# Forgetting attention with a gelu feed-forward block: row-tiled causal masks, a reordered batch 0, and batch 1 in the steady order

## The chip, the cores and the metric

The kernel runs on one core of a Trainium2 chip. The metric is the device time of one execution in microseconds (us), median of several executions. Before the change it is 352.60 us (four runs beside those of the changed kernel, 352.09 to 354.32).

## The reference, cut to what matters

```python
# q, k, v: (8 batches, 8 heads, 576 tokens, 64); f: (8, 8, 576)
cum    = cumsum(log(clip(f, 1e-4, 1)))
scores = q @ k.T / 8 + cum[:, None] - cum[None, :]      # causal: -1e9 above the diagonal
x      = (softmax(scores) @ v), as (4608 tokens, 512)
h      = x @ w_in                                        # (512, 2048)
out    = (0.5 * h * (1 + erf(h / sqrt(2)))) @ w_out      # exact gelu; w_out (2048, 512)
```

So each batch needs attention, a first product with gelu, and a second product. The decay by f is folded into v (a weight for each token), so the scores need only the causal mask.

## The kernel before

Heads are handled in pairs (HP = 4 pairs a batch). The scores of a pair are four tiles of up to 448 columns per head, each followed by one exponential on ScalarE. TensorE interleaves batch b's attention with single products of batch b-1's second product ("fill"). From batch 2 on, q and k are transposed by DMA; batches 0 and 1 transpose them on TensorE, because their loads come too late for that.

The causal mask is put on by TensorE itself in batch 0 and for pair 0 of batch 1: a 128-row product of the identity with a mask tile opens the accumulation, and the score piece is cut in two around the masked 128 columns. Elsewhere GpSimd masks after the exponential.

```python
def scores(b, i, t):
    on_pe = b == 0 or (b == 1 and i == 0)
    for x, c in enumerate(SDIAG[t] if on_pe else []):        # masked columns of this tile
        for h in range(2):
            nc.tensor.matmul(st[:, h, c:c+P], ident_bf, after, start=x == 0, stop=False)
    for n, q0, w in STILES[t]:
        cut = P if on_pe and c in SDIAG[t] and w > P else w
        for a0, a1 in ((0, cut), (cut, w)):
            for h in range(2 if a1 > a0 else 0):             # two heads on 64 rows each
                nc.tensor.matmul(st[:, h, c+a0:c+a1], kT[i][d, ...], qT[i][d, ...], ...)
    nc.scalar.activation(et, st, Act.Exp, scale=scale)
```

One block of transposes for a pair of heads of batch 1 is twelve TensorE transposes (q, then k, two 64-wide tokens side by side) and eight VectorE copies out of PSUM, four for qT and then four for kT:

```python
def transposes_pe(b, i, pool):
    for src, ps in zip(qk_of[b], pss):                       # q, then k
        for h in range(2):
            for j in range(JT // 2):
                nc.tensor.transpose(ps[:, h, j, :], src[:, 2*i+h, 2*j*D:2*(j+1)*D], ...)
    for which, ps in enumerate(pss):                         # qT, then kT
        for h in range(2):
            for odd in range(2):
                nc.vector.tensor_copy(rows[:, odd], ps[odd*D:(odd+1)*D, h]...)
```

Before, three of these blocks stand in batch 0's first product and the fourth early in batch 1's attention. The first quarter of w_out is loaded after batch 0's attention, the other three in the middle of its first product.

The softmax here doesn't subtract the row's maximum and nothing guards it: scores larger than these inputs give would overflow.

## Time and profile before

| what | value | from |
|---|---|---|
| median of the timed runs | 352.60 us | 4 runs |
| the profiled execution | 355.01 us, span 352.8, mean clock 0.985 | a run of its own, none of those four |
| TensorE busy | 96% of the span | the page |
| batch 0's attention (from the transposes of heads 2 and 3 to its first product) | 9.55 to 29.65 | stages |
| batch 0's first product | 16.67 us | stages |
| batch 1's attention with batch 0's second product | 27.24 us | stages |
| the same pair of stages in the steady state | 22.89 us | stages |

The stages are cut where the first matmul of each starts. TensorE is the engine that sets the time, so the reading goes by its waits and its granted clock. The lines themselves stand in the prediction below.

### The profile page before, as it was taken

The numbers are of one execution on the slowest core, as the hardware profiler recorded it, in microseconds if no ns is written. First come the engines' busy times: TensorE is split into PE (matmuls) and PEld (weight loads), VectorE is DVE, ScalarE is ACT, GpSimd is POOL, SyncE is SP. The second block draws the span as 40 slices with busy tenths as digits, with TensorE's granted clock in tenths as the row PEclk, the third lists the DMA queues.
The fourth block names the chain that finished last, engine by engine and source line by source line (L and its number), as shares of the span: only waits on it lengthen the run. The fifth ranks groups of instructions, "written<-read, shape, count | busy, mean of one in ns | idle before, by whom it ended". The sixth has DMA issues, their size and how long they took to land.

```text
span 352.8 us, 7762 instructions
## 1 busy us (share of the span) xinstructions
PE 338.2 (96%) x3080; PEld 177.0 (50%) x3122; DVE 203.6 (58%) x501; ACT 215.3 (61%) x296; POOL 124.4 (35%) x243
## 2 busy tenths in 40 slices
PE   6898989999999999999999999999999999999995
PEld 3564544544555455544554455445544554444443
DVE  4363785499358945795579566965697463011011
ACT  6567676536874687468746875687657864603600
POOL 7291066235446234532455144614360530000000
PEclk9679999999999999999999999999999999999999
DMA  7899989965987989287926894589710121011013
GB/s 111 175 169 191 202 140 198 186 140 142 191 148 177 134 160 201 69 127 147 215 75 112 122 212 124 90 146 202 139 39 0 46 65 64 2 59 59 2 30 89
DMA packets 101219, 43.24 MB, mean 123 GB/s; under 512 B 80000, under 2 KB 96640, under 8 KB 101184
## 3 DMA queue, kind: packets, MB, share of 16 engines
q1 hardware_dynamic: 83888, 28.60, 39.2%
q0 software_dynamic: 16896, 13.63, 25.8%
q8 instruction: 24, 0.39, 0.5%
q10 hardware_dynamic: 400, 0.52, 0.4%
q14 instruction: 11, 0.09, 0.1%
HBM read 36.85 MB, written 9.44 MB: 131 GB/s over the span
## 4 chain that ended last, share of the span: by engine, by line
PE 85%; ACT 9%; issue 2%; DMA 2%; POOL 1%; DVE 0%; ACTq 0%; POOLq 0%
PE ps L398 35%; PE ps L487 17%; PE ps L438 11%; PE o L335 10%; PE s L304 8%; ACT e L314 5%; ACT L314 2%; ACT g L411 2%; DMA k<-in_k_dram 2%; PE s L295 1%; PE ps_f L192 1%; PE ps_x L373 1%; PE ps_t L220 0%; PE s_t L220 0%; POOL q L102 0%
## 5 line engine op out<-in xcount | busy, mean ns | idle before, releaser
L411 ACT ACTIVATE g<-ps 128x512 bf16<-128x512 f32 x144 | 85.8, 597 | 83.4 <-PE ps L398 83.4
L314 ACT ACTIVATE e<-s 128x896 bf16<-128x896 f32 (+1 forms) x128 | 104.1, 862 | 33.9 <-PE s L304 33.1
L398 PE MATMUL ps<-xT,w_in_sb 128*128 128x512 bf16 x502 | 112.0, 380 | 1.6 <-ACT g L411 1.0
L487 PE MATMUL ps<-w_out_sb,g 64*128 64x512 bf16 (+1 forms) x666 | 96.2, 377 | 1.0
L316 POOL TENSOR_SCALAR_AFFINE_SELECT e<-e 128x256 bf16<-128x256 bf16 x135 | 53.5, 406 | 116.7 <-ACT e L314 115.5
L398 PEld LDWEIGHTS <-w_in_sb 128*128 128x128 bf16 x576 | 56.0, 98 | 68.0 <-issue 3.2
L279 POOL TENSOR_TENSOR vw<-v_sb,wT 128x640 bf16<-128x640 f32 x32 | 40.9, 1278 | 47.1 <-DMA v_sb<-in_v_dram 31.0
L304 PE MATMUL s<-qT,kT 64*128 64x320 bf16 (+5 forms) x424 | 48.1, 280 | 2.6 <-ACT e L314 2.0
L487 PEld LDWEIGHTS <-g 64*128 64x128 bf16 (+1 forms) x690 | 37.7, 94 | 25.4 <-issue 1.6
L335 PEld LDWEIGHTS <-e 128*128 128x128 bf16 x960 | 36.1, 98 | 18.1 <-issue 11.3
L263 DVE COPY qT<-tq 64x288 bf16<-64x288 bf16 x96 | 43.4, 452 | 1.5
L438 PE MATMUL ps<-w_out_sb,g 128*128 128x512 bf16 (+2 forms) x201 | 43.3, 363 | 0.3
L335 PE MATMUL o<-vw,e 128*128 128x65 bf16 x960 | 42.3, 196 | 0.8 <-ACT e L314 0.4
L495 DVE COPY ot<-ps 128x512 f32<-128x512 f32 x24 | 16.5, 689 | 36.0 <-PE ps L487 36.0
L447 DVE COPY ot<-ps 128x512 f32<-128x512 f32 (+2 forms) x13 | 8.4, 650 | 48.9 <-PE ps L438 46.0
L263 DVE COPY kT<-tk 64x288 bf16<-64x288 bf16 x96 | 34.0, 354 | 1.6
L304 PEld LDWEIGHTS <-kT 64*128 64x128 bf16 x424 | 20.2, 96 | 26.4 <-issue 14.4
L350 DVE RECIPROCAL r<-o 128x5 f32<-128x5 f32 x64 | 12.5, 195 | 30.8 <-PE o L335 29.8
L351 DVE TENSOR_TENSOR x<-o,r 128x256 bf16<-128x256 f32 x64 | 27.2, 425 | 2.2
L438 PEld LDWEIGHTS <-g 128*128 128x128 bf16 x208 | 18.7, 98 | 19.1 <-issue 0.6
L361 DVE TENSOR_SCALAR xt<-o,r 64x64 bf16<-64x64 f32 x60 | 17.4, 290 | 1.4
L497 DVE TENSOR_TENSOR ot<-ot,ps 128x512 f32<-128x512 f32 x24 | 16.5, 688 | 1.3
(61 smaller groups left out, 147.2 us busy)
## 6 DMA issues: line engine op xcount, KB each, us to landing
out_dram<-ot SPq DMA_DIRECT2D x32, 256.0 KB, 2.1
v_sb<-in_v_dram SPq DMA_DIRECT2D x20, 256.0 KB, 4.6
v_sb<-in_v_dram SPq DMA_DIRECT2D x29, 128.0 KB, 6.0
q<-in_q_dram POOLq DMA_DIRECT2D x6, 576.0 KB, 6.2
k<-in_k_dram POOLq DMA_DIRECT2D x6, 576.0 KB, 8.2
w_in_sb<-in_moe_w_in_dram POOLq DMA_DIRECT2D x4, 512.0 KB, 7.6
w_out_sb<-in_moe_w_out_dram POOLq DMA_DIRECT2D x4, 512.0 KB, 8.7
q<-in_q_dram POOLq DMA_DIRECT2D x4, 144.0 KB, 5.4
```

The source lines that it names most:

```text
L263: nc.vector.tensor_copy(rows[:, odd], src[odd * D : (odd + 1) * D, 2 * i + h].rearrange("d j p -> d p j"),)
L279: nc.gpsimd.tensor_tensor(vw_of[b][:, hs, :, 0:D], v_sb[:, hs, :, :], w.unsqueeze(3).to_broadcast([P, 2, NBLK, D]), Alu.mult,)
L304: nc.tensor.matmul(st[:, h, c + a0 : c + a1], kT[i][d, K0[n] : K0[n] + P], qT[i][d, q0 + a0 : q0 + a1], start=not on_pe, stop=not on_pe or ...
L314: nc.scalar.activation(et[:, :, 0:c], st[:, :, 0:c], Act.Exp, scale=scale)
L316: nc.gpsimd.affine_select(out=et[:, :, c0 : c0 + P], in_=et[:, :, c0 : c0 + P], compare_op=Alu.is_ge, fill=0.0, base=0, pattern=[[0, 2], [ ...
L335: nc.tensor.matmul(o[:, m, :], e_of[b, i, t][:, h, c : c + P], vw_of[b][:, 2 * i + h, n, :], start=(n == 0), stop=(n == m),)
L351: nc.vector.tensor_tensor(x_of[b, i][:, :, h, :], o[:, 0:4, 0:D], r[:, 0:4].unsqueeze(2).to_broadcast([P, NBLK - 1, D]), Alu.mult,)
L361: nc.vector.tensor_scalar(*tail, r[D:P, 4:5], None, Alu.mult)
L398: nc.tensor.matmul(ps, w_in_sb[:, kt, ffb * P : (ffb + 1) * P], src[:, kt, :], start=(kt == 0), stop=(kt == n_dm - 1),)
L411: nc.scalar.activation(g_of[c][ffb], ps, Act.Gelu)
L438: nc.tensor.matmul(pss[ts][:, c0:c1], g_of[c][kt][:, ts * P : (ts + 1) * P], w_out_sb[:, kt, c0:c1], start=(kt == 0), stop=(kt == n_ff - 1),)
L487: nc.tensor.matmul(banks[r], g_of[c][kt][rows, ts * P : (ts + 1) * P], w_out_sb[rows, kt, :], start=(kt == 0), stop=last if r else kt == n ...
```

## The change

Its intent: make batch 0's masks cheaper and its order tighter, so that everything after starts sooner; give batch 1 the order that the later batches have; and bring the weights in an order in which batch 0's second product works on two token blocks at once, one quarter of w_out after another. In exchange the last two pairs' q and k of batch 1 arrive later and are transposed inside batch 1's attention.

```diff
     def scores(b, i, t):
-        on_pe = b == 0 or (b == 1 and i == 0)
+        on_pe = b == 0 or (b == 1 and i < 2)
...
+            masked = on_pe and c in SDIAG[t]
+            for half in range(-1, 2 if masked else 0):
+                for h in range(2):
+                    if half < 0:      # the whole score piece
+                        to = st[:, h, c : c + w]
+                        ab = kT[i][d, ...], qT[i][d, ...]
+                    else:             # 64 mask rows, 64 or 128 columns
+                        to = st[:, h, c : c + last]
+                        ab = key_of[d, half, :], after[d, half, 0:last]
... batch 0: q,k of heads 2,3 loaded one place earlier; score tiles one place ahead of
    transposes and attends; then the loads
+        load_v(1, 0, 4)
+        load_v(1, 4, 8)
+        load_qk_tokens(1, 0, 4)
+        load_w_in(2)
+        load_w_in(3)
+        load_w_out(0)
+        load_w_out(1)
+        load_qk_tokens(1, 4, 8)
+        load_w_out(2)
+        load_w_out(3)
... batch 1
-    FILL_1 = [[0, 4, 4, 0], [0, 2, 3, 3], [4, 4, 4, 4], [3, 3, 3, 3], [8, 0, 99]]
+    FILL_1 = [[2, 2, 2, 2], [2, 2, 2, 2], [2, 3, 4, 4], [3, 4, 4, 4], [8]]
     def second_attention():
+        fill = gemm2_first(0)         # two token blocks by quarters of w_out, then rows
         for i in range(HP):
             for t in range(4):
                 scores(1, i, t)
+                take(fill, FILL_1[i][t])
                 if i and t == 1:
+                    av(i - 1)
...
+                if (i, t) in ((1, 2), (2, 2)):
+                    transposes_pe(1, i + 1, s_psum)
...
         for ffb in range(0 if b else 4, n_ff):
             gemm1(b, ffb)
             if b == 0:
-                if ffb in (6, 8, 13):
+                if ffb in (7, 10):
                     transposes_pe(...)
```

More of the change, by code (lines that the diff above doesn't have):

```diff
@@ L121 @@
     load_qk_tokens(0, 0, 2)
+    load_qk_tokens(0, 2, 4)
     ident_bf = consts.tile([P, P], BF16)
     make_identity(nc, ident_bf)
-    load_qk_tokens(0, 2, 4)
     load_qk_tokens(0, 4, 6)
-    after = consts.tile([P, P], BF16)
-    nc.gpsimd.memset(after, 0.0)
-    nc.gpsimd.affine_select(
-        out=after,
-        in_=after,
-        compare_op=Alu.is_ge,
-        fill=-1.0e9,
-        base=0,
-        pattern=[[1, P]],
-        channel_multiplier=-1,
-    )
+    key_of = consts.tile([P, 2, P], BF16)
+    after = consts.tile([P, 2, P], BF16)
+    for t, op, fill in (
+        (key_of, Alu.not_equal, 1.0), (after, Alu.is_ge, -1.0e9)
+    ):
+        nc.gpsimd.memset(t[0:D], 0.0)
+        nc.gpsimd.affine_select(
+            out=t[0:D],
+            in_=t[0:D],
+            compare_op=op,
+            fill=fill,
+            base=0,
+            pattern=[[-D, 2], [1, P]],
+            channel_multiplier=-1,
+        )
     nc.gpsimd.memset(v_sb[:, :, 0, 0:1], 0.0)
@@ L289, in scores @@
     def scores(b, i, t):
-        on_pe = b == 0 or (b == 1 and i == 0)
+        on_pe = b == 0 or (b == 1 and i < 2)
         st = s_psum.tile([P, 2, 512], FP32, tag="s", name=f"s{t}")
-        for x, c in enumerate(SDIAG[t] if on_pe else []):
-            for h in range(2):
-                nc.tensor.matmul(
-                    st[:, h, c : c + P], ident_bf, after, start=x == 0, stop=False
-                )
-        c, width = 0, sum(w for _, _, w in STILES[t])
+        c = 0
         for n, q0, w in STILES[t]:
-            cut = P if on_pe and c in SDIAG[t] and w > P else w
-            for a0, a1 in ((0, cut), (cut, w)):
-                for h in range(2 if a1 > a0 else 0):
+            masked = on_pe and c in SDIAG[t]
+            for half in range(-1, 2 if masked else 0):
+                for h in range(2):
                     d = slice(h * D, (h + 1) * D)
-                    nc.tensor.matmul(
-                        st[:, h, c + a0 : c + a1],
-                        kT[i][d, K0[n] : K0[n] + P],
-                        qT[i][d, q0 + a0 : q0 + a1],
-                        start=not on_pe,
-                        stop=not on_pe or c + a1 == width,
+                    if half < 0:
+                        to = st[:, h, c : c + w]
+                        ab = kT[i][d, K0[n] : K0[n] + P], qT[i][d, q0 : q0 + w]
+                    else:
+                        last = (half + 1) * D
+                        to = st[:, h, c : c + last]
+                        ab = key_of[d, half, :], after[d, half, 0:last]
+                    nc.tensor.matmul(
+                        to, *ab, start=half < 0, stop=half == 1 or not masked
                     )
@@ L465, with gemm2_first, gemm2_rows @@
     ]
-    def gemm2_rows(c):
-        for ts, steps in enumerate(STEPS):
+    def gemm2_first(c):
+        pss = [
+            m_psum.tile([P, d_model], FP32, tag="m", name="ps2") for _ in range(2)
+        ]
+        for kq in range(4):
+            for ts in range(2):
+                for kt in range(4 * kq, 4 * kq + 4):
+                    nc.tensor.matmul(
+                        pss[ts],
+                        g_of[c][kt][:, ts * P : (ts + 1) * P],
+                        w_out_sb[:, kt, :],
+                        start=(kt == 0),
+                        stop=(kt == n_ff - 1),
+                    )
+                    if kt == n_ff - 1:
+                        ot = o_pool.tile([P, d_model], FP32, tag="ot", name="ot")
+                        nc.vector.tensor_copy(ot, pss[ts])
+                        nc.sync.dma_start(
+                            out[c * S + ts * P : c * S + (ts + 1) * P, :], ot
+                        )
+                    yield
+        yield from gemm2_rows(c, 2)
+    def gemm2_rows(c, ts0=0):
+        for ts in range(ts0, n_sub):
+            steps = STEPS[ts]
             if ts < n_sub - 1:
@@ L521, in first_attention @@
         transposes(0, o_psum, "o")
+        nc.vector.tensor_copy(key_of[D:P], key_of[0:D])
+        nc.vector.tensor_copy(after[D:P], after[0:D])
         warm_up(4)
         scores(0, 0, 0)
+        scores(0, 0, 1)
         transposes(1, m_psum, "m")
-        scores(0, 0, 1)
+        scores(0, 0, 2)
         psw = o_psum.tile([P, NBLK, BH], FP32, tag="o", name="psw")
@@ L530, in first_attention @@
             )
+        scores(0, 0, 3)
         nc.vector.tensor_copy(wT[:, 0:4, :], psw[:, 0:4, :])
         nc.vector.tensor_copy(wT[D:P, 4, :], psw[D:P, 4, :])
-        scores(0, 0, 2)
-        scores(0, 0, 3)
+        scores(0, 1, 0)
         transposes(2, m_psum, "m")
-        scores(0, 1, 0)
         scores(0, 1, 1)
@@ L540, in first_attention @@
         scores(0, 1, 3)
-        weigh_v(0, 0)
-        load_w_in(0)
-        load_w_in(1)
-        weigh_v(0, 1)
-        load_qk_tokens(1, 0, 4)
-        weigh_v(0, 2)
-        weigh_v(0, 3)
-        load_w_in(2)
-        load_w_in(3)
+        for i in range(HP):
+            weigh_v(0, i)
+            if i < 2:
+                load_w_in(i)
         nc.gpsimd.memset(v_sb[:, :, 0, 0:1], 0.0)
@@ L552, in first_attention @@
         load_v(1, 4, 8)
+        load_qk_tokens(1, 0, 4)
[3 more added lines that the diff above has]
+        load_w_out(1)
         load_qk_tokens(1, 4, 8)
+        load_w_out(2)
+        load_w_out(3)
         scores(0, 2, 0)
+        scores(0, 2, 1)
+        scores(0, 2, 2)
         attend_head(0, 0)
-        scores(0, 2, 1)
+        scores(0, 2, 3)
         attend_head(0, 1)
-        scores(0, 2, 2)
-        scores(0, 2, 3)
+        scores(0, 3, 0)
         attend_head(1, 0)
-        scores(0, 3, 0)
+        scores(0, 3, 1)
         attend_head(1, 1)
+        scores(0, 3, 2)
         to_xT(0, 0, nc.vector.tensor_copy)
-        scores(0, 3, 1)
-        scores(0, 3, 2)
+        scores(0, 3, 3)
         attend_head(2, 0)
-        scores(0, 3, 3)
         attend_head(2, 1)
@@ L629, in second_attention, with av @@
     def second_attention():
-        b, fill, counts = 1, gemm2(0, True), FILL_1
+        fill = gemm2_first(0)
+        def av(i):
+            for h in range(2):
+                attend(1, i, h, (0, 1, 2, 3, 4))
+                if h == 0:
+                    take(fill, FILL_AV[i])
+                normalize(1, i, h)
         for i in range(HP):
             for t in range(4):
-                scores(b, i, t)
+                scores(1, i, t)
+                take(fill, FILL_1[i][t])
                 if i and t == 1:
-                    attend(b, i - 1, 0, (0, 1, 2))
-                elif i and t == 2:
-                    attend(b, i - 1, 0, (3, 4))
-                    normalize(b, i - 1, 0)
-                elif i and t == 3:
-                    attend(b, i - 1, 1, (0, 1, 2, 3, 4))
-                    normalize(b, i - 1, 1)
-                    if i < HP - 1:
-                        x_dma(b, i - 1)
-                if (i, t) == (0, 2):
-                    transposes_pe(1, 3, o_psum)
-                if i == 1 and t in (0, 2):
-                    weigh_v(1, 2 + t // 2)
-                if t == 3:
-                    if i == 1:
-                        load_v(2, 0, 4)
-                    if i == 2:
-                        transpose_dma(2, 0, 4)
-                take(fill, counts[i][t])
@@ L654, in second_attention @@
-        i = HP - 1
-        take(fill, counts[HP][0])
-        to_xT(b, i - 1, nc.vector.tensor_copy, o_psum, "o")
-        attend(b, i, 0, (0, 1, 2, 3, 4))
-        normalize(b, i, 0)
-        take(fill, counts[HP][1])
-        attend(b, i, 1, (0, 1, 2, 3, 4))
-        normalize(b, i, 1)
-        take(fill, 7)
-        to_xT(b, i, nc.vector.tensor_copy, o_psum, "o")
-        x_tail_dma(b)
+                    av(i - 1)
+                    if i < HP - 1:
+                        x_dma(1, i - 1)
@@ new lines, in second_attention @@
+                if (i, t) in ((1, 1), (2, 0)):
+                    weigh_v(1, i + 1)
+                if (i, t) in ((1, 2), (2, 2)):
+                    transposes_pe(1, i + 1, s_psum)
+                if (i, t) == (2, 1):
+                    load_v(2)
+                if (i, t) == (3, 0):
+                    transpose_dma(2, 0, 4)
+        take(fill, FILL_1[HP][0])
+        to_xT(1, HP - 2, nc.vector.tensor_copy, o_psum, "o")
+        av(HP - 1)
+        take(fill, 5)
+        to_xT(1, HP - 1, nc.vector.tensor_copy, o_psum, "o")
@@ L665, in second_attention @@
+        x_tail_dma(1)
         transpose_dma(2, 4, 8)
-        load_v(2, 4, 8)
         take(fill, 999)
@@ L676 @@
         if b == 0:
-            load_w_out(0)
             x_tail_dma(0)
@@ L681 @@
             if b == 0:
-                if ffb in (6, 8, 13):
-                    transposes_pe(
-                        1, (6, 8, 13).index(ffb), s_psum if ffb < 10 else o_psum
-                    )
-                if ffb == 9:
+                if ffb in (7, 10):
+                    transposes_pe(1, (7, 10).index(ffb), s_psum)
+                if ffb == 12:
                     weigh_v(1, 0)
-                    for c in range(1, 4):
-                        load_w_out(c)
                     load_qk_tokens(2)
```

## The prediction

> **What bounds the kernel now.** I read the page first, then busy time by stage (stages cut where the first matmul of each starts), then TensorE's timeline, the clock per microsecond, and VectorE's timeline around the transposes of q and k.
>
> ```profile
> PE 338.2 (96%) x3080; PEld 177.0 (50%) x3122; DVE 203.6 (58%) x501; ACT 215.3 (61%) x296; POOL 124.4 (35%) x243
> ```
>
> TensorE is busy 96% of the span, so time comes only from TensorE work removed, TensorE waits, or its clock. The stages (columns: window, its length, busy us of PE, PEld, DVE, ACT, POOL with counts, granted clock, DMA share, GB/s):
>
> ```profile
> 0.00:9.55 9.55, 6.02 (x49) 2.71 (x49) 3.93 (x7) 5.46 (x6) 7.01 (x19) 1.00 0.82 120
> 9.55:29.65 20.10, 19.45 (x318) 13.44 (x320) 10.75 (x27) 14.03 (x19) 12.12 (x18) 0.75 1.02 172
> 29.65:46.32 16.67, 15.55 (x102) 7.82 (x104) 9.87 (x23) 10.15 (x17) 2.74 (x4) 1.00 1.09 181
> 46.32:73.56 27.24, 25.30 (x267) 12.75 (x270) 17.11 (x44) 16.49 (x19) 15.19 (x29) 1.00 1.03 177
> 73.56:87.47 13.91, 13.86 (x63) 6.17 (x65) 13.38 (x33) 8.96 (x15) 4.68 (x7) 1.00 0.65 149
> 87.47:110.36 22.89, 22.38 (x289) 13.09 (x292) 12.01 (x33) 16.06 (x19) 9.15 (x21) 1.00 1.03 176
> ```
>
> In order: start; batch 0's attention; its first product (gelu input); batch 1's attention with batch 0's second product; then the same pair in the steady state. Only the first four can change. Batch 0's attention runs at clock 0.75 on average, and batch 1's attention costs 27.24 against the steady 22.89. The clock per microsecond is 1.00 to 11, 0.68 in 11:12, 0.50 from 12 to 21, 0.71 in 21:22, then 1.00. Ahead of the fall stands this gap, and inside it the masks:
>
> ```profile
> 9.55 0.47 PE L192 MATMUL ps_f<-ident_bf,k 96*64 96x96 bf16 x10 [1.59 <-DMA k<-in_k_dram]
> 13.85 0.61 PE L295 MATMUL s<-after,ident_bf 128*128 128x128 bf16 x4
> 14.39 0.56 PE L304 MATMUL s<-qT,kT 64*128 64x128 bf16 x8
> 14.88 0.39 PE L295 MATMUL s<-after,ident_bf 128*128 128x128 bf16 x2
> 23.53 0.38 PE L295 MATMUL s<-after,ident_bf 128*128 128x128 bf16 x4
> 23.85 0.37 PE L304 MATMUL s<-qT,kT 64*128 64x128 bf16 x8
> 24.15 0.65 PE L335 MATMUL o<-vw,e 128*128 128x65 bf16 x15
> 87.47 0.37 PE L304 MATMUL s<-qT,kT 64*128 64x256 bf16 x4
> 87.67 1.46 PE L487 MATMUL ps<-w_out_sb,g 64*128 64x512 bf16 x12
> ```
>
> Read the distance between starts: score tile 0 with its masks takes 14.88-13.85 = 1.03 us at half clock, 24.15-23.53 = 0.62 at full, and unmasked in the steady state 87.67-87.47 = 0.20. That last one is 448 columns per head, both heads side by side on 64 rows.
>
> **What the Trainium skill says.** (1) "TensorE: Matmul & The Clock Gate", part 1: an idle window of some 3.4 us halves TensorE's clock, a busy one restores it, and windows run free of the kernel. The trace agrees in kind: half clock for about 10 us, three such windows. But it fell after a gap of 1.59 us followed by transposes, so less than a whole idle window is enough. (2) "TensorEngine Tiling (Array Packing)", Key Properties: a change of tiling mode drains the array. The trace agrees: the 64x256 score tile takes 0.30 between full-array products in batch 1 (56.49 to 56.78), 0.20 above. So I take 0.1 us per switched tile. (3) "VectorE: DVE Perf Modes", Why PSUM operands drop a tier: a PSUM source is capped at a slower mode. The same 64x288 copies take 480 ns for kT and 478 ns for qT from PSUM here, against 354 and 452 ns from SBUF.
>
> **The change, part by part.**
>
> *Masks and order of batch 0: a gain.* A masked pair of heads had ten 128-row mask matmuls and four extra score pieces; now the scores run whole and each of five masks is two 64-row pieces of 64 and 128 columns, heads side by side, with no mode switch. Columns per pair of heads for the four tiles: 832, 640, 640, 512. At 2.4 columns per ns (448/2.4 = 187 ns, the 0.20 above) that is 1.09 us, at half clock 2.19. Before: 0.62+0.51+0.51+0.45 = 2.09 at full clock, 1.03+0.90+0.80+0.71 = 3.44 at half. So 1.0 to 1.25 us are saved for each of four head pairs: 4.0 to 5.0 of TensorE work. Besides, q and k of heads 2,3 are issued one DMA pair's place earlier (about 0.6 us), and a second score tile runs before their transposes, so ScalarE's second exponential moves from 10.93 to about 9.
>
> ScalarE's floor: twelve exponentials of 0.93 and four of 0.70 = 13.9 us from 8.1, plus gaps of 1 to 2, ends at 23 to 24. Walking the new TensorE order with half clock still from 11.3 to 21.5, I get the last attend at 25.2; warm from 18, 24.2; cold throughout, 27. Choice: 25.2 in place of 29.65, **-4.4 us**. The two added VectorE copies of the mask tiles (about 0.25 each) come while ScalarE still copies the first qT: nothing.
>
> *First product of batch 0.* Two transpose blocks in it, not three: 0.51 each (12 transposes, 37.17 to 37.68): **-0.5**. The weights must keep up: 0.52 MB per quarter as written. Between 28 and 42 us the DMA moves 194 GB/s, of which v takes 67 (1.18 MB in 17.7 us), leaving 127. Counting the new queue from 17 us (w_in 0, 1, q,k, w_in 2, 3, w_out 0, 1, q,k, w_out 2, 3): w_in 2 lands near 33.5 (needed 34.1), w_in 3 near 37.9 (needed 38.1), w_out 0 near 41.6 (needed 41.8), w_out 2 near 50. Just in time; I add **+0.5**.
>
> *Batch 1's attention: a loss.* The last two head pairs' q,k arrive late and are transposed inside the attention, for pair 2 after its predecessor's third score tile, for pair 3 likewise. What one block costs VectorE:
>
> ```profile
> 37.01 0.42 PE L220 MATMUL s_t<-ident_bf,q 96*128 96x96 bf16 x6
> 37.26 0.42 PE L220 MATMUL s_t<-ident_bf,k 96*128 96x96 bf16 x6
> 37.72 1.95 DVE L232 COPY qT<-s_t 64x288 bf16<-64x288 bf16 x4 [5.85 <-PE s_t L220]
> 39.69 1.95 DVE L232 COPY kT<-s_t 64x288 bf16<-64x288 bf16 x4
> ```
>
> So 1.95+1.95 = 3.9 us of copies, and their score tile cannot start before them: the new instruction order shows that the weight load of kT there waits for VectorE. Between block and score tile TensorE has, for pair 2, one masked tile (0.31) and two products (0.43): stall 4.0-0.75 = 3.2. For pair 3 one tile (0.25) and four products (0.86), with VectorE also evicting an output block (0.69, partly beside): stall 3.0. The next row-split product needs a PSUM bank whose eviction stands behind those copies: 0.3. Before, all blocks lay three or more microseconds ahead of use.
>
> The rest, walked with these durations: old masks on pair 0 (2.09) become 1.09; pair 1 gains masks on TensorE (+0.4; its five selects leave POOL, off the path); one more transpose block (+0.5); the start of the stage stays bound by the last gelu, the table load and two exponentials (third score tile 3.08 us after the first, as now); 64 products of 0.216 and eight attends of about 0.5 stay. My walk without stalls gives 27.1, against 27.24 now: no gain. With 3.2+3.0+0.3: **+6.4**.
>
> *Clock after the two stalls.* Each is twice the gap that halved the clock in batch 0, but dense products stand on both sides, so it depends on where the windows fall. A window at half clock costs some 1.7 us; at a bit over one in all, **+2.0**. Where one cold window contains the second stall it costs less.
>
> Sum: 352.2 - 4.4 - 0.5 + 0.5 + 6.4 + 2.0 = 356.2. The clock term is the least known and may be zero, so I put the time at 355.5.
>
> **Rivals.** (a) The stalls do not bite and batch 0's gain stands: 347 to 348. For it: the change looks built around its DMA order, and batch 0's masks are surely cheaper. Against: in-order TensorE, 3.9 us of measured copies, under 1.3 us of work between. (b) DMA becomes the bound: 6.5 MB at about 190 GB/s from 17 us end near 52, so work on the last weight quarter cannot begin sooner however fast batch 0 is. Its waits would partly lie under the stalls; if weights lag 2 us: 357. (c) The clock falls in both stalls and stays low for several windows, as in batch 0: 360. (d) Batch 0 never falls to half clock, ScalarE bounds it, 24 us, and no stall cools the array: 352.
>
> **Range and chances.** The extremes of (d) and (c) give 350.5 to 360.5. Faster by over 2% (under 345.2) needs (a) and more: 0.05. Slower by over 2% (above 359.3) needs (c) or DMA lag on top: 0.18. Within 2%: 0.77.
>
> **What would show it.** Right: the first product starts near 25; a masked head pair's four score tiles take about 1.1 us of TensorE at full clock; in batch 1's attention TensorE waits twice for VectorE's qT/kT copies, about 3 us each, in front of the first score tiles of pairs 2 and 3, and that stage lasts 33 to 36 us; from batch 1's first product on, all durations as before. Wrong: a first product still after 28 (the clock, or v, decided batch 0); waits for w_in or w_out over 1 us; or a batch 1 attention under 29 us, which would mean that the copies are hidden and the stall step is false.

## The result, and the profile after

| | before | after |
|---|---|---|
| median | 352.60 us (352.09 to 354.32, 4 runs) | 363.58 us (363.02 to 364.05, 4 runs) |
| ratio | | 1.0302, 95% interval 1.0262 to 1.0341: slower |

A ratio, here and below, is the mean time of one kernel's fast runs over that of the other's of the same rounds, so it is not quite the ratio of the medians. The prediction of 355.5 us was wrong, and its range ended at 360.5.

The page of the changed kernel, its line of busy times and its line of granted clock in 40 slices of 9 us:

```profile
PE 340.1 (94%) x3131; PEld 178.1 (49%) x3174; DVE 205.3 (57%) x505; ACT 215.2 (60%) x296; POOL 123.5 (34%) x240
...
PEclk9999996899999999999999999999999999999999
```

TensorE works as much as before (340.1 against 338.2) in a longer span (361.1 against 352.8), and the clock is low in the seventh and eighth slice, 54 to 72 us, not in batch 0. The stages (batch 0's attention, its first product, batch 1's attention, the rest; columns as in the prediction; the first cut differs from that of the kernel before, since at 8.95 the first score tile is under way):

```profile
8.95:25.66 16.71, 15.03 (x338) 12.18 (x335) 10.66 (x27) 14.46 (x20) 10.59 (x17) 1.00 0.97 167
25.66:41.91 16.25, 15.18 (x90) 7.21 (x91) 8.63 (x20) 10.22 (x17) 7.90 (x11) 1.00 1.24 198
41.91:80.97 39.06, 30.53 (x321) 15.60 (x327) 18.59 (x48) 16.66 (x19) 8.41 (x17) 0.87 0.98 158
80.97:361.10 280.13, 271.98 (x2350) 140.14 (x2382) 162.90 (x403) 169.21 (x236) 89.03 (x178) 1.00 0.58 107
```

Batch 0's first product starts at 25.66, near the predicted 25.2, but batch 1's attention takes 39.06 us and TensorE works in only 30.53 of them. (This execution also began slowly: four warm-up products take 1.89 us from 6.92 on, 1.04 in the kernel before, and products run at half speed until about 10.6, though the clock column says 1.00 there.) TensorE's timeline there (start, busy time, instructions merged in a row; in brackets the wait ahead of them and what ended it):

```profile
52.72 0.43 PE L226 MATMUL s_t<-ident_bf,k 96*128 96x96 bf16 x6 [1.49 <-DMA k<-in_k_dram]
...
54.95 0.58 PE L479 MATMUL ps<-w_out_sb,g 128*128 128x512 bf16 x1 [1.47 <-DMA w_out_sb<-in_moe_w_out_dram]
56.17 0.39 PE L311 MATMUL s<-qT,kT 64*128 64x256 bf16 x1 [0.64 <-DVE kT L238]
57.17 0.55 PE L311 MATMUL s<-qT,kT 64*128 64x256 bf16 x3 [0.61 <-DVE kT L238]
...
67.23 0.28 PE L311 MATMUL s<-qT,kT 64*128 64x256 bf16 x1 [1.90 <-DVE kT L238]
68.23 0.28 PE L311 MATMUL s<-qT,kT 64*128 64x256 bf16 x2 [0.72 <-DVE kT L238]
```

The three last kinds of line are the two predicted stalls: the first score tile of pair 2 (56.17, 57.17) and of pair 3 (67.23, 68.23) waits for VectorE's kT. The copies behind the first of them, on VectorE, are of the predicted length:

```profile
53.19 1.95 DVE L238 COPY qT<-s_t 64x288 bf16<-64x288 bf16 x4 [2.03 <-PE s_t L226]
55.15 1.96 DVE L238 COPY kT<-s_t 64x288 bf16<-64x288 bf16 x4
```

Two things in the timeline were not in the prediction's sum. The transposes of k wait 1.49 us for their load, and a product waits 1.47 us for w_out. The second wait costs nothing of its own, since it lies beside the copies, from 53.5 to 55.0, and kT comes only at 57.1. A third comes at the end of the stage, where batch 1's first product waits 0.98 us for xT, whose copy VectorE does last (the first line is TensorE's, the second VectorE's):

```profile
82.76 13.33 PE L401 MATMUL ps<-xT,w_in_sb 128*128 128x512 bf16 x60 [0.98 <-DVE xT L379]
```

```profile
82.29 0.42 DVE L379 COPY xT<-ps_x 128x512 bf16<-128x512 bf16 x1
```

Two steps of an output block, 0.69 us each, stand ahead of that copy on VectorE from 80.96 on, and TensorE has no fill left to do beside them.

Last, the clock. Cut into windows of 3.41 us so that edges fall where the clock changes:

```profile
51.58:54.99 3.41, 0.80 (x13) 0.63 (x14) 1.76 (x4) 0.70 (x1) 1.45 (x2) 1.00 1.13 175
54.99:58.40 3.41, 2.16 (x7) 0.43 (x7) 2.05 (x5) 0.59 (x1) 0.00 (x0) 0.50 1.27 195
...
65.23:68.64 3.41, 0.79 (x6) 0.30 (x6) 3.29 (x7) 0.00 (x0) 0.41 (x1) 1.00 0.97 201
68.64:72.06 3.42, 3.17 (x18) 1.36 (x16) 0.26 (x1) 1.83 (x2) 0.99 (x3) 0.50 1.25 259
```

A window in which TensorE is busy for 0.8 us of 3.41 is followed by half clock: after the first stall for two windows (the next, 58.40 to 61.82, is at 0.50 as well), after the second for one.

### The profile page after: what moved, and what is told of

Same layout as the page of the kernel before. It is cut to its first block, busy times and chain, and to the rows that moved or that the text cites. A ratio compares the mean times of both kernels' runs of the same rounds, so it can differ in the third digit from the quotient of the medians.

```text
span 361.1 us, 7859 instructions
## 1 busy us (share of the span) xinstructions
PE 340.1 (94%) x3131; PEld 178.1 (49%) x3174; DVE 205.3 (57%) x505; ACT 215.2 (60%) x296; POOL 123.5 (34%) x240
## 4 chain that ended last, share of the span: by engine, by line
PE 73%; DMA 7%; ACT 7%; POOL 4%; DVE 4%; issue 2%; SPq 2%; POOLq 0%; ACTq 0%
PE ps L401 30%; PE ps L516 19%; PE o L338 8%; PE ps L441 8%; DMA k<-in_k_dram 7%; PE s L311 6%; ACT e L317 4%; ACT L317 2%; SPq L114 2%; DVE kT L238 1%; DVE qT L238 1%; POOL q L102 1%; ACT g L414 1%; POOL w_in_sb L161 1%; PE ps L479 1%
## 5 line engine op out<-in xcount | busy, mean ns | idle before, releaser
L516 PE MATMUL ps<-w_out_sb,g 64*128 64x512 bf16 (+1 forms) x718 | 105.9, 380 | 1.4 <-DVE ot L488 0.2
L319 POOL TENSOR_SCALAR_AFFINE_SELECT e<-e 128x256 bf16<-128x256 bf16 x130 | 51.6, 406 | 133.0 <-ACT e L317 131.6
L311 PE MATMUL s<-qT,kT 64*128 64x320 bf16 (+4 forms) x384 | 49.5, 288 | 7.9 <-DVE kT L238 3.9
L516 PEld LDWEIGHTS <-g 64*128 64x128 bf16 (+1 forms) x744 | 41.0, 95 | 29.7 <-issue 3.9
L269 DVE COPY qT<-tq 64x288 bf16<-64x288 bf16 x96 | 45.1, 470 | 1.4
L524 DVE COPY ot<-ps 128x512 f32<-128x512 f32 x26 | 17.9, 690 | 35.6 <-PE ps L516 35.6
L269 DVE COPY kT<-tk 64x288 bf16<-64x288 bf16 x96 | 32.2, 336 | 3.4 <-DMA tk<-k 1.8
L450 DVE COPY ot<-ps 128x512 f32<-128x512 f32 (+2 forms) x9 | 5.7, 632 | 48.7 <-PE ps L441 46.0
L441 PE MATMUL ps<-w_out_sb,g 128*128 128x512 bf16 (+2 forms) x141 | 27.8, 355 | 0.2
L441 PEld LDWEIGHTS <-g 128*128 128x128 bf16 x144 | 13.5, 98 | 14.5
```

What stands on the lines that cost most here:

```text
L269: nc.vector.tensor_copy(rows[:, odd], src[odd * D : (odd + 1) * D, 2 * i + h].rearrange("d j p -> d p j"),)
L311: nc.tensor.matmul(to, *ab, start=half < 0, stop=half == 1 or not masked)
L319: nc.gpsimd.affine_select(out=et[:, :, c0 : c0 + P], in_=et[:, :, c0 : c0 + P], compare_op=Alu.is_ge, fill=0.0, base=0, pattern=[[0, 2], [ ...
L441: nc.tensor.matmul(pss[ts][:, c0:c1], g_of[c][kt][:, ts * P : (ts + 1) * P], w_out_sb[:, kt, c0:c1], start=(kt == 0), stop=(kt == n_ff - 1),)
L516: nc.tensor.matmul(banks[r], g_of[c][kt][rows, ts * P : (ts + 1) * P], w_out_sb[rows, kt, :], start=(kt == 0), stop=last if r else kt == n ...
L524: nc.vector.tensor_copy(ot, banks[1])
```

## The experiments

Four theories were open after the result: that the copies in front of pairs 2 and 3 make the stage long; that the clock behind them does; that late loads do; and that batch 0's gain was never there, or was given back.

**Is the gain of batch 0 real on its own?** `b0_only`: the kernel before with only batch 0's part (masks, the earlier q and k, the new order of tiles); loads of weights and batch 1 as before.

```diff
 # before, with these alone
-            nc.tensor.matmul(st[:, h, c : c + P], ident_bf, after, ...)
+            ab = key_of[d, half, :], after[d, half, 0:last]      # as in the change
+    load_qk_tokens(0, 2, 4)                                      # ahead of the identity
 ... and the order of scores, transposes and attends of batch 0
```

> The kernel before with batch 0's part of the change alone (row-tiled masks, q,k of heads 2,3 loaded first, new order of batch 0's tiles), batch 1 and the order of the weight loads as before. Theory A (the batch 0 part gains what the traces show, 29.65 to 25.66, and batch 1 loses it): first product of batch 0 starts at 25.5 to 26, batch 1's attention stays near 27 to 29 us, time 348 to 350. The median run of before was some 2.5 us shorter than its profiled run, so the gain on the median may be only 1 to 3 us. Rival B (an earlier batch 0 only makes the weights late): time within 1 us of before, with the gain returned as waits for w_in or w_out.

Measured: 353.46 us, ratio 1.0008 (0.9948 to 1.0067): same. The first product does start at 25.27, and batch 1's attention at 42.25, but that stage then takes 30.34 us. Its longest wait on TensorE:

```profile
50.69 1.01 PE L439 MATMUL ps<-w_out_sb,g 128*128 128x512 bf16 x2 [1.67 <-DMA w_out_sb<-in_moe_w_out_dram]
```

Two waits for exponentials of 1.20 and 0.67 us come before it and half clock from 50.7 to 54.1 after it. So the start was moved forward and the time given back one stage later, as rival B had it.

**Which late load?** `tail_late`: the changed kernel, with the small DMA transpose of batch 0's last 64 tokens ("tails", needed only at the very end) issued during batch 1's pair 3 rather than right after batch 0.

```diff
                 if (i, t) == (3, 0):
                     transpose_dma(2, 0, 4)
+                    x_tail_dma(0)
-        if b == 0:
-            x_tail_dma(0)
```

> The changed kernel with the DMA transpose of batch 0's tails issued 20 us later, after the weights. Theory A (that transpose, issued into the full queue, holds DMA engines up from 47 to 52 us, and so the last k of batch 1): the wait of 1.5 us for k goes, v's second half lands before 50, batch 1's attention ends 1.5 to 2.5 us earlier, time 361 to 362. Rival B (the queue is simply that long): no packets of 4 us go away or the wait for k stays, time as the changed kernel, 363.6 within 0.5.

Measured: 363.09 us, ratio 1.0278, against 1.0302 for the change: above the 361 to 362 of theory A, and the two intervals overlap. The wait for k is gone and the stage is 37.8 us long instead of 39.06, but its profiled execution had half clock in batch 0 (18.5 to 21.9) and so reached the stage 1.9 us later, which alone would let k arrive in time. The cleaner evidence is that of the DMA engines. How long the tails' transpose took from issue to landing, first in the kernel before, then in the changed one (the view of DMA issues):

```profile
tails<-xt SPq DMA_TRANSPOSE x1, 2.4
```

```profile
tails<-xt SPq DMA_TRANSPOSE x1, 15.7
```

In the changed kernel it is issued into a full queue, and between 50 and 52 us, just before k is wanted, the DMA moves 67 GB/s (last column). In `mended` below, which also issues it late and comes to its transposes sooner, at 49.56, it moves 206 in the same stretch (201 in `tail_late`), and the transposes don't wait:

```profile
50.00:52.00 2.00, 1.23 (x16) 0.68 (x14) 1.06 (x4) 0.92 (x1) 0.00 (x0) 1.00 1.03 67
```

```profile
50.00:52.00 2.00, 0.91 (x22) 0.76 (x18) 1.73 (x4) 1.35 (x2) 0.46 (x1) 1.00 1.24 206
```

So the wait for k comes of the tails' transpose. Its removal gains little time here, since the copies and the clock behind it stay.

**What is the clock worth?** `warm_fill`: the changed kernel, with thirteen products without use in each of the two gaps, ahead of the real ones, so that TensorE is busy but gets no result sooner.

```diff
                 scores(1, i, t)
+                if (i, t) in ((1, 3), (2, 3)):
+                    idle = o_psum.tile([P, TC], FP32, tag="o", name="ps_d")
+                    for _ in range(13):
+                        nc.tensor.matmul(idle, warm[:, 0:P], warm, start=True, stop=True)
```

> The changed kernel with 13 dummy products of 512 columns in each of the two gaps in which TensorE waits for the copies of kT and qT of pairs 2 and 3. Theory A (the two gaps halve the clock for about 10 us, which costs 3.8 us): clock 1.00 throughout batch 1, the waits for the copies stay in place, time 359.5 to 360.5. Rival B (the clock's cost is only what was in the prediction, 2 us): 361.5. Rival C (the half clock comes from the wait for k before, which is not filled): clock still falls, time 363.6.

Measured: 360.12 us, ratio 1.0193 (0.0109 below the change, 3.8 us of 353; by the medians 3.5). The clock is at 1.0 throughout, and batch 1's attention lasts from 41.85 to the product below, 76.98, 35.13 us: 3.93 less, with 26 products more. Of these, 0.4 are not the clock's: k was there earlier in this execution (its wait is 1.06 us, not 1.49). The clock is thus worth some 3.5 us.

```profile
76.98 0.81 PE L401 MATMUL ps<-xT,w_in_sb 128*128 128x512 bf16 x3
```

The interval of the ratio, 1.0149 to 1.0237, leaves the verdict against the kernel before unclear at 2%; against the change it is plain.

**What are the copies worth?** `split_copy` was to take half of them off VectorE: kT of pairs 2 and 3 is copied by ScalarE.

```diff
-                    nc.vector.tensor_copy(
+                    op = nc.scalar.copy if which and i >= 2 else nc.vector.tensor_copy
+                    op(
```

> The changed kernel with the four kT copies of pairs 2 and 3 on ScalarE, beside the four qT copies on VectorE. Theory A (the 3.9 us of copies in front of pairs 2 and 3 set the path): each gap shortens by 1.5 to 2 us, 3 to 4 in all, and the clock may then stay up for a further 2 to 4: time 356 to 360.5. Rival B (late weights or a full ScalarE set the path): under 1 us gained, with the waits for the copies replaced by waits for w_out or for the exponentials.

Measured: 363.52 us, ratio 1.0292, no gain. It does not speak against the copies, because the edit did not do what it was meant to. ScalarE's line:

```profile
56.01 1.97 ACT L239 COPY kT<-s_t 64x288 bf16<-64x288 bf16 x4 [4.17 <-DVE qT L239]
```

ScalarE waited for VectorE's copies of qT, which read the same PSUM tile, and then took as long as VectorE would have. The two ran one after the other.

`quick_T` shortens the copies instead: pairs 2 and 3 are transposed head by head and token by token, 24 transposes of 64 columns in place of 12 of 128, so that qT and kT each leave PSUM in one copy on 128 partitions rather than four on 64.

```diff
+    def transposes_late(b, i):
+        for which, src in enumerate(qk_of[b]):
+            for h in range(2):
+                for j in range(JT):
+                    nc.tensor.transpose(ps[h*D:(h+1)*D, j, :], src[:, 2*i+h, j*D:(j+1)*D], ...)
+        for which in range(2):
+            nc.vector.tensor_copy((qT, kT)[which][i]..., both[:, which, 0:S]...)
-                    transposes_pe(1, i + 1, s_psum)
+                    transposes_late(1, i + 1)
```

> The changed kernel with q and k of pairs 2 and 3 transposed head by head, as batch 0 does it, so that two copies of about 0.75 us take the place of eight of 0.48; 0.3 us more of transposes each. Theory A (the copies in front of pairs 2 and 3 are on the path, and the gaps that they make also cost the clock): each gap shortens by 2.0 to 2.3 us, and the half clock goes from the second one at least: 4 to 8 us gained, 355.5 to 359.5. Rival B (late w_out and k set the path there): the first gap keeps its length, waits for w_out in place of waits for the copies; 361 or more.

Measured: 356.97 us (355.76 to 357.82), ratio 1.0102 (1.0059 to 1.0145): 6.6 us faster than the change by the medians, 7.1 by the ratios. VectorE's copies of pair 2, and the score tile that they hold up:

```profile
53.60 0.76 DVE L256 COPY qT<-s_l 128x576 bf16<-128x576 bf16 x1 [2.72 <-PE s_l L250]
54.28 0.75 DVE L256 COPY kT<-s_l 128x576 bf16<-128x576 bf16 x1
```

```profile
56.07 0.56 PE L329 MATMUL s<-qT,kT 64*128 64x256 bf16 x4 [0.36 <-issue]
```

The copies take 1.5 us instead of 3.9, no product or score waits over 0.4 us for them, and half clock remains only from 54.1 to 60.9 (behind waits of 1.82 for k and 1.24 for w_out). The second fall of the clock is gone with the second stall. Stalls and the clock behind them thus belong together.

**Can all be mended?** `mended`: `quick_T`, with the tails late and another distribution of the fill, which was to leave a product or two for the end.

```diff
-    FILL_1 = [[2, 2, 2, 2], [2, 2, 2, 2], [2, 3, 4, 4], [3, 4, 4, 4], [8]]
+    FILL_1 = [[4, 4, 0, 1], [2, 2, 0, 3], [2, 3, 2, 6], [3, 4, 4, 4], [9]]
...  take(fill, 4) ahead of the last transposes, x_tail_dma(0) as in tail_late
```

> quick_T with the tails' DMA transpose after the weights, eight products of the first weight quarter in the opening two tiles of batch 1, more products beside the shorter copies, and one product left behind the last transpose of x so that its copy is not behind two evictions. Theory A (copies, clock, the blocked DMA engines and that last wait account for the loss): batch 1's attention 28 to 29.5 us, no half clock in it, time 351 to 353, about as before. Rival B (there is a further cost in the steady order or in the weights): attention above 31 us, time 354 or more, with waits for w_out on TensorE.

Measured: 356.60 us (354.81 to 359.55), ratio 1.0102: no better than `quick_T`. In its profiled execution, the fastest of its runs, batch 1's attention takes 29.16 us and ends at 70.43, 0.6 ahead of the kernel before when that is warm (71.07, below), and the clock is full. So this part of theory A held, and its 351 to 353 us did not. The fill was miscounted (all of it is used before the last transposes, as in the change), so the wait for xT stayed at 1.05 us, and batch 2's attention got a new wait of 2.38 us. That one stands in the chain behind a DMA transpose of batch 2's k that took 12 us. It looks as if what was gained in batch 1 is asked of batch 2's loads, but no run separates that.

**Was the clock of batch 0 part of the time before?** `before_again` is the kernel before, profiled once more without a change.

> The kernel before, unchanged, for a second profile. Its timed runs have spans from 350.1 us at clock 0.999 to 352.9 at 0.995 or less, and the profiled run had 352.8 at 0.985. Theory A (the profile that the prediction was worked out on is the slow kind: half clock for 10 us in batch 0, which most runs do not have): clock 1.00 through batch 0, first product of batch 0 at 26.5 to 27.5 instead of 29.65, span 350 to 350.7. Rival B (the runs differ elsewhere): first product near 29.6 again whatever the clock.

Measured: 354.94 us, span 352.6, clock 0.985, half clock from 11.63 to 21.87, first product at 29.49: the same kind of execution again. It doesn't decide, since two profiled executions say nothing of the unprofiled ones beside them, five of which, out of seven, had clock 0.998 to 1.0 and spans of 349.8 to 351.6.

`b0_warm` decides it: the kernel before, with eight products without use in the gap ahead of the transposes of heads 2 and 3.

```diff
         scores(0, 0, 0)
+        warm_up(8)
         transposes(1, m_psum, "m")
```

> The kernel before with eight dummy products in batch 0's gap in front of the transposes of heads 2,3 (1.22 to 1.59 us in the two profiles). Theory A (that gap sets off the half clock of 10 us, which the two profiled runs have and most timed runs lack): clock 1.00 through batch 0 in the profile, first product of batch 0 at 26.5 to 27.5 instead of 29.5, span 350 to 350.7; time like the quicker runs of before, 352 to 352.8, with less spread. Rival B (the half clock has another cause, the transposes or the sparse work after): half clock again, first product at 29 or later.

`masks_only`: the kernel before with the new masks and nothing else.

```diff
-            nc.tensor.matmul(st[:, h, c : c + P], ident_bf, after, ...)
+            ab = key_of[d, half, :], after[d, half, 0:last]
```

> The kernel before with the row-tiled masks alone (order of batch 0, loads and batch 1 as before). Theory A (the masks are 4 to 5 us of TensorE work in batch 0, but at full clock ScalarE's exponentials bound batch 0): four masked score tiles take 1.1 us per head pair at full clock; first product 1 to 2.5 us earlier than the 27 or so of a warm run of before; time 350.5 to 352.5, unless late weights take it back as in b0_only. Rival B (all of the masks' work was on the path): first product at 25.5, time 348 to 349.

Measured: `b0_warm` 353.18 us, ratio 1.0015 (0.9958 to 1.0072); `masks_only` 353.02 us, ratio 0.9992 (0.9950 to 1.0034). Both same. Their first products of batch 0, in this order:

```profile
26.68 1.02 PE L398 MATMUL ps<-xT,w_in_sb 128*128 128x512 bf16 x4
```

```profile
26.70 1.02 PE L399 MATMUL ps<-xT,w_in_sb 128*128 128x512 bf16 x4
```

A warm execution of the kernel before thus starts its first product at 26.7, not 29.65, and takes as long in all (span 350.3) as the faster timed runs of the kernel before. The clock is not all that spreads those runs: `b0_warm`'s own still go from 352.52 to 355.18, not with the smaller spread that was expected, and one of the kernel before had a span of 352.1 at clock 0.999.

`masks_only` missed theory A: it starts its first product no earlier, though its masks are cheaper. Its profile alone doesn't say what they are worth at full clock, since TensorE comes to the first attend sooner, waits there for GpSimd's weighted v, and one window (17.1 to 20.5) is at half clock behind that:

```profile
16.94 0.89 PE L336 MATMUL o<-vw,e 128*128 128x65 bf16 x15 [1.35 <-POOL vw L289]
```

But another of its runs, at clock 1.0, has a span of 350.4, so at full clock too the masks alone bring nothing in all. What holds the stage when the masks are cheaper is shown less well. Besides that wait for v, one of the last attends of both kernels waits 0.40 us for an exponential, and in the changed kernel ScalarE's sixteen exponentials run from 9.65 to 23.42 with gaps of only 0.17, 0.21 and 0.29: that speaks for ScalarE setting the pace there, but no run tests it.

**Where is batch 0's remaining microsecond lost?** Two experiments on `b0_only` give the weights more of a lead. `b0_weights` has all four quarters of w_out right behind the last q and k, with the tails late. `b0_w_out1` has only the second quarter moved behind the first.

```diff
 # b0_weights
         load_qk_tokens(1, 4, 8)
+        for c in range(4):
+            load_w_out(c)
```

> The run b0_only with all four quarters of w_out issued straight after the last q,k of batch 1 instead of after the first weighted v, and the tails' DMA transpose after them. Theory A (late weights and the half clock behind that wait gave back what batch 0's part gained): the wait of 1.67 us for w_out and the 3.4 us of half clock go, time 349.5 to 351. Rival B (the gain was not there, since the runs of before mostly have no half clock in batch 0): time 352 to 353.5.

```diff
 # b0_w_out1
             load_w_out(0)
+            load_w_out(1)
             x_tail_dma(0)
...
-                    for c in range(1, 4):
+                    for c in range(2, 4):
                         load_w_out(c)
```

> b0_only with the second quarter of w_out issued right behind the first instead of behind batch 1's first weighted v. Theory A (the wait of 1.67 us for that quarter, and the 3.4 us of half clock that follow it, gave back batch 0's gain): both go, v is late by less than its slack of some 5 us; batch 1's attention 27 to 28 us instead of 30.3, time 349.5 to 351, quicker than before by 0.5 to 0.9%. Rival B (any load moved ahead only makes v or q,k late, as in b0_weights): time 352.5 or more, with waits of the attends for the weighted v or the selects behind it.

Measured: `b0_weights` 362.73 us, ratio 1.0268, outside both theories; `b0_w_out1` 354.03 us (six runs), ratio 1.0020 (0.9985 to 1.0054), as its rival B had it. In the first, TensorE waits for GpSimd's masks:

```profile
62.18 0.35 PE L336 MATMUL o<-vw,e 128*128 128x65 bf16 x3 [7.81 <-POOL e L317]
```

GpSimd, in order, was itself held by a weighted v whose load the weights had delayed. In the second the same thing shows in small (GpSimd's timeline):

```profile
47.54 1.27 POOL L283 TENSOR_TENSOR vw<-v_sb,wT 128x640 bf16<-128x640 f32 x1 [18.52 <-DMA v_sb<-in_v_dram]
```

In `b0_only` this weighted v starts at 43.40. The wait for the second quarter is gone, one of 1.46 for the next quarter and one of 1.41 for GpSimd's masks are there instead. In these two runs, moving one load ahead delayed another.

**And the wait for xT?** `last_left`: the changed kernel with one fill product fewer ahead of the last transposes, so that one is left for after them. Not timed in rounds.

```diff
-    FILL_1 = [..., [3, 4, 4, 4], [8]]
+    FILL_1 = [..., [3, 4, 4, 4], [7]]
```

> The changed kernel with one product of batch 0 fewer before batch 1's last attends, so that one is left after the last transpose of x (as in the steady batches). Theory A (the wait of 0.98 us in front of batch 1's first product is VectorE's: two evictions of the last output block stand ahead of the copy of xT): the wait falls under 0.2 us. Rival B (xT's copy is late for another reason): the wait stays at 0.9 to 1.0.

Measured: 363.51 us, span 361.7. The wait is gone: the copy of xT starts at 81.25, ahead of the two steps of the output block. Every later stage then starts 0.84 us earlier than in the change, to the last product, which ends at 356.76 and not 357.60. The total hides this, since the last write of the output took longer in this one execution. The last issues of the change and of `last_left`, from issue to landing:

```profile
out_dram<-ot ACTq DMA_DIRECT2D x1, 32.0 KB, 2.1
```

```profile
out_dram<-ot ACTq DMA_DIRECT2D x1, 32.0 KB, 3.6
```

So this wait is worth 0.84 us on TensorE, and the single total can neither show nor refute it.

No experiment beats the kernel before. The best of the changed line, `mended` and `quick_T`, are 1% slower.

## Why the prediction was wrong, and where it was right

The comparison to make is that of a warm execution of the kernel before, `b0_warm`, span 350.3, with the changed one, span 361.1. Batch 0's first product and batch 1's attention in `b0_warm`:

```profile
26.68:43.33 16.65, 15.63 (x109) 7.81 (x106) 9.80 (x23) 10.21 (x17) 0.26 (x2) 1.00 1.17 192
43.33:71.07 27.74, 26.01 (x273) 12.91 (x272) 17.37 (x46) 16.74 (x20) 17.93 (x32) 1.00 1.14 171
```

| term | predicted | measured | how |
|---|---|---|---|
| start and batch 0's attention | -4.4 | -1.0 | 25.66 - 26.68 |
| first product, with its loads | -0.5 + 0.5 | -0.4 | 16.25 - 16.65 |
| batch 1's attention: stalls, and all else in it | +6.4 | +6.3 | what is left of 39.06 - 27.74 without the next two rows |
| half clock behind them | +2.0 | +3.5 | `warm_fill`'s stage, less the earlier k |
| wait for k | none | +1.5 | the line at 52.72 |
| wait for xT, and the rest | none | +0.9 | 280.13 - 279.23 (350.3 - 71.07) |
| sum | +4.0 | +10.8 | 361.1 - 350.3 |

*The stalls: right.* From the end of pair 2's transposes to its score tile are 4.0 us, copies of 1.95 and 1.96 as predicted, and pair 3 likewise (4.1). The walk gives 33.6 for the stage (27.1 without stalls, and 3.2 + 3.0 + 0.3). The stage's 39.06, less the wait for k of 1.5 and the clock of 3.5, is 34.1; the masks of pair 0, which take 1.56 there and not 1.09, come to nearly that difference. `quick_T` shows that the copies, with the clock that they bring, are 6.6 us of the loss.

*Batch 0: the step that failed worst.* "25.2 in place of 29.65, -4.4 us" came close with its first number (25.66) and failed with its second. The 29.65 belongs to an execution with half clock from 11.35 to 21.59, but the sum starts from 352.2, a median of three runs whose clock is not on record; of the fifteen timed runs of the same kernel in later rounds, fourteen had a clock of 0.995 or more, which leaves no room for such a stretch (0.985 in the profiled one). The times at hand said so: the profiled execution is 2.8 us above that median, at clock 0.985. Rival (d) held that batch 0 does not fall to half clock, but only of the changed kernel, and set it at 352 without seeing that the base then moves as well. Against a warm run the part is worth 1.0 us in the changed kernel's profile with its slow beginning, and 1.4 to 1.8 in `quick_T`, `warm_fill` and `mended`, which have the same batch 0 (25.25, 25.18 and 24.86).

That 25.2 came close is partly luck. It was walked with half clock from 11.3 to 21.5, which the changed kernel did not have, and with masks cheaper than they are. At full clock the four tiles of pair 3 take 0.47 + 0.39 + 0.38 + 0.33 = 1.57 us there (from 19.41 to 22.46, each to the product behind it), not 1.09: the sum left out the 0.1 us that the prediction itself sets for a switched tile (0.12 each here). So a pair's masks save 0.5 us of TensorE work against the 2.09 before, 2.1 in batch 0 and not 4.0 to 5.0, and `masks_only` shows none of it in the total. Two small readings: 56.49 to 56.78 is 0.29, not 0.30, and the 0.51 of a transpose block stands from 37.01 to 37.52.

*The clock: the mechanism right, the size off.* "At a bit over one in all, +2.0" was three windows, 10.24 us at half clock, and 1.2 us each, not 1.7. From the two timelines: from pair 2's score tile to the end of pair 3's transposes are 6.95 us in the changed kernel (57.17 to 64.12) and 4.89 in `warm_fill`; from the end of pair 3's copies to the end of the stage 12.80 and 11.28; together 3.6. The ratios give 3.8, the medians 3.5. Rival (c), the clock in both stalls, named 360 and was the closest.

*The loads: "just in time" was wrong for k.* The order of landing was worked out from bytes at an even rate. The k of pairs 2 and 3 was there only at 52.7, while the DMA moved 67 GB/s in the two microseconds from 50 on. The count had no place for a DMA transpose in a full queue, which took 15.7 us and held them up; `tail_late` and `mended` show the wait gone without it. The prediction's test "waits for w_in or w_out over 1 us" came true for w_out as well, 1.47, but beside the copies, where it cost nothing in this kernel.

*The wait for xT* was not foreseen. That the last fill product ends ahead of the last transposes could have been counted from the code: `last_left` removes it by one number.

The trace also agrees with one thing that the prediction used only in a rate. It gave v a share by bytes measured in the kernel before. The Trainium skill, "DMA: Bandwidth & Descriptors", section "Queues, rings and completion order", says that each engine takes turns between the queues that have work, a packet at a time. Between 40 and 48 us of the changed kernel the GpSimd queue and the hardware queue moved 1386 and 1382 packets, but 1.17 and 0.34 MB: equal turns, unequal bytes. So a load of small packets slows its neighbour by packets, and its share of bytes is not what to plan by.

A faster start of batch 0 was given back to late loads in the three kernels tried on `b0_only`'s side; that is not shown for every order that could be written. Whether an order of loads exists that keeps the microsecond of batch 0 stays open.

## What to carry to other kernels

Before a term is costed from a profile, compare the profiled execution's time and clock with those of the timed runs: a stage that is slow only in the profiled one cannot be gained. Between a transpose on TensorE and its first user stand the copies out of PSUM, and a stall that leaves TensorE mostly idle for a window is paid again as half clock behind it; either put work between, or shape the transposes so that the copies use all partitions. And when a load is moved ahead, name the load that it delays.

## What the Trainium skill lacked or had wrong

- "TensorE: Matmul & The Clock Gate", part 1, has the clock fall after an idle window of some 3.4 us; of shorter idle stretches it says, under "A second HAM failure mode: psum-queue depth-cycling", only that frequent ones made the clock swing in another kernel, without a figure. Here it fell after windows in which TensorE was busy for 0.80 and 0.79 of 3.41 us (changed kernel), 1.38 (`quick_T`, 50.69 to 54.10) and 1.96 (`masks_only`, 13.69 to 17.10). A window need not be idle; how busy it must be, no page and no run here says.
- The same part has the clock restored after one busy window or more. In the changed kernel one was enough (3.42 of 3.42 us busy from 58.40 to 61.82, then full clock). In the kernel before TensorE was busy for 3.41 of 3.41 us from 11.35 to 14.76 and for 3.23 from 14.76 to 18.18, with transposes and short score pieces, and the clock stayed at half until 21.59. What sort of work counts as busy there, no run here tells.
- "DMA: Bandwidth & Descriptors" ("Rules for kernel authors") says that a DMA transpose needs no care next to ordinary DMAs, which is about correctness, and has nothing on its cost to them. Issued into a full queue it took 15.7 us instead of 2.4, and the whole core's DMA fell to 67 GB/s for 2 us where it moves 206 without it.
